# A chunked recurrence ahead of two dense layers: Gram products later, one subtraction moved to TensorE, copies in another order

## The chip, the cores and the metric

One NeuronCore of a Trainium2 chip runs the whole program. Its engines work from queues of their own and wait for each other by semaphores: TensorE (PE; its weight loads are PEld), VectorE (DVE), ScalarE (ACT), GpSimd (POOL) and SyncE (SP), which issues the DMAs. The metric is the device time of one execution in microseconds (us), median of several.

## What is computed

Three layers follow each other. For 4 batches, 8 heads, 768 tokens and a head size of 48, the first keeps a 48 x 48 state per head:

```python
k_n = k / (norm(k) + 1e-6)
for t in range(768):
    y[t]  = q[t] @ state
    v_old = k_n[t] @ state
    state = state + beta[t] * outer(k_n[t], v[t] - v_old)
```

The second takes x (the heads side by side, 384 wide): `theta = x @ w_theta`, `u = x + w_tok_r @ (x cos theta) + w_tok_i @ (x sin theta)`, `u + relu(u @ w_ch)`. The third is a layer norm with a two-layer network of width 1536 and a residual. Inputs and outputs are float32; some weights come as 64-bit floats and are rebuilt on the chip.

## The kernel before

**Chunks.** The recurrence is done in 24 chunks of 32 tokens, for 32 heads (batch x head) at once, in two halves h of 16. Within a chunk the tokens are coupled by the Gram matrix of their keys; its triangular inverse `PT`, once per group s of 4 chunks (6 groups), is computed from the keys alone. For chunk c and half h the steps are: `R` (TensorE forms K S, S being the state, and a subtraction gives `Rs = V - K S`), `W_mm` (PT times Rs), `W_out` (four ScalarE copies to `bdw`), `S` (TensorE adds K^T W to the state in PSUM, and two ScalarE copies give `bds` for the next chunk). `yq_work` and `ym_work` form the output Y, one ScalarE copy takes it to `ys`, and four DMAs take it to x.

**Gram products.** `a_work(c)` is the set for chunk c: 16 products on TensorE, two ScalarE copies (to `G_sb` for the inverse and to `MT` for the output), a mask on GpSimd. The first eight chunks' sets are made ahead of the loop. `spread` loads the keys in block form (`bdk`) two chunks ahead of a set.

**Inverse.** `inverse_work(s)` gives three lists (A, B, C) of DVE instructions, with some products on GpSimd: a transposition of the Gram blocks (`tg`, from `G_sb` to `Gi`, only when the sets of all four chunks are done), norms with a ScalarE square root between DVE instructions, the rows of 8 x 8 inverses, the steps to 16 and 32, and the transposition to `PT`. `Stream` hands them out: each half of a chunk calls `dv.run(budget)`, which emits instructions until their written-down cost passes the budget; list C of one group is mixed with list A of the next as far as that one is ready, and what a run can't emit is not carried over. In the fourth chunk of a group, and in chunk 18, the rest is emitted until PT of the next group exists.

**Order on the engines.** Each engine runs its instructions in the order in which the program writes them. In chunk c: K S of half 0 and its subtraction, inverse work, part of a Gram set, S of half 1 of the chunk before, W of half 0, Y of the chunk before, K S of half 1 and its subtraction, inverse work, the rest of the Gram set, S of half 0, W of half 1. From chunk 18 on, `late(c, k)` puts in the first work of the next layer at three places of a chunk: weights are loaded and rebuilt on DVE (`wts.step`: two instructions or three), and two tiles are prepared (`trans`, `theta`, `angles`, `sines`, `cosines`, `turn`, `rest`: x is transposed by TensorE and copied to xh and xl, its sines and cosines times x are zf, split into zh and zl). After the attention the loop over 24 tiles `mix(i, half)` begins on TensorE, with the preparation of later tiles and weights between.

Of the kernel before, what the change touches and what calls it, by code (L numbers as in the profile page):

```python
# [6 lines left out]
F32 = mybir.dt.float32  # L7
# [85 lines left out]
def attention(ctx, tc, kq, ktok, vin, betai, maskin, x, psa, late=None):  # L93
# [20 lines left out]
    beta = cst.tile([128, NS, 32], F32, name="beta")  # L114
    NB = 3
# [128 lines left out]
    def inverse_work(s):  # L244
# [10 lines left out]
        def op(n, fn, w=None, wait=0.13):  # L255
            (w or A).add(0.068 + n / 960.0, fn, wait)
# [19 lines left out]
        def n2():  # L276
            for nm in ("s1", "sh", "rc", "n", "bp", "nb"):
                nrm[nm] = sm(nm)
            v.tensor_scalar(out=nrm["s1"], in0=nrm["s0"], scalar1=1e-30, scalar2=None, op0=ALU.max)

        n2.ready = lambda: ("n1", s) in done
        op(32, n2, wait=0.4)
        op(192, lambda: v.reciprocal(out=nrm["rc"], in_=nrm["s1"]))
        op(32, lambda: v.tensor_scalar(out=nrm["sh"], in0=nrm["s1"], scalar1=0.5, scalar2=1e-6, op0=ALU.mult, op1=ALU.add), wait=0.0)
# [18 lines left out]
        A.add(0.0 if s > 1 else 0.33, lambda: (nc.gpsimd if s > 1 else v).tensor_tensor(out=N8, in0=g8[:, :, :, 0:8],  # L303
# [127 lines left out]
    def R(h, c):  # L431
        if c == 0:
            return V[0][:, 4 * h:4 * h + 4, :]
        b = bds[h][c % 2]
        for g in range(2):
            for r in range(4):
                nc.tensor.matmul(RW[h][32 * r:32 * r + 32, 0, 2 * g:2 * g + 2, :], KQ[c][:, 0, 2 * h + g, r, :],
                                 b[:, 4 * g + r, :, :], start=True, stop=True)
        Rs = p2.tile([128, 4, D], F32, name=f"Rs{h}")
        nc.vector.tensor_tensor(out=Rs, in0=V[c][:, 4 * h:4 * h + 4, :], in1=RW[h][:, 0, :, :], op=ALU.subtract)  # L440
        return Rs
# [75 lines left out]
    one = ecst.tile([128, 1], F32, name="one")  # L517
# [86 lines left out]
    for c in range(1, NC):  # L604
        s = c // 4
        step[0] = c
        load_kq(c + 11)
        load_v(c + 5)
        scale_v(c + 2)
        load_kt(c + 2)  # L610
        wa, wm, wq = Work(), Work(), Work()
        for n in {1: (9, 10), 2: (11, 12)}.get(c, (c + 10,)):
            if n < NC:
                a_work(wa, n)
        ym_work(wm, c - 1)
        yq_work(wq, c)
        R0 = R(0, c)
        budget = 2.3 if c >= 14 else 3.08
        if c % 4 == 1 and c > 1 and s + 1 < NS:
            while ("tg", s + 1) not in done:  # L620
                dv.step()
        dv.run(budget)
        if late:
            late(c, 0)
        wa.run((0.0 if c == 2 else 0.42) * wa.left())
        S(1, c - 1)
        W(0, c, R0)
# [24 lines left out]
    pe.flush()
# [472 lines left out]
def build(tc, a):  # L1125
# [8 lines left out]
    with tc.manual_schedule(), outer:  # L1134
        gp = outer.enter_context(tc.tile_pool(name="glob", bufs=1, **R))
        ident = gp.tile([128, 128], F32, name="ident")
        ones = gp.tile([128, 128], F32R, name="ones")
# [53 lines left out]
        with ExitStack() as att:  # L1191
            attention(att, tc, a["kq"], a["ktok"], a["vin"], a["betai"], a["mask"], x, psa, late)
# [4 lines left out]
        ff.ones = ones  # L1197
# [150 lines left out]
```

## Time and profile before

| | us |
|---|---|
| median of 3 runs (lowest, highest) | 784.87 (784.21, 785.08) |
| profiled execution, its own time | 786.73 |
| its span in the trace | 784.80 |
| busy: PE, DVE, ACT, POOL | 709.4, 517.8, 356.9, 213.2 |
| mean granted clock of PE | 0.969 |

The span is from the first to the last instruction in the trace; what the time has beyond it lies outside of the instructions. Busy times of engines overlap, so they don't add up to the span.

### The profile page before, as it was taken

The page shows a single profiled execution, that of the slowest core. Times are in us where ns is not written, and L with a number is a line of the kernel's source. Part 1 is how long each engine was busy: PE and PEld are TensorE (multiplying, and loading weights), DVE is VectorE, ACT ScalarE, POOL GpSimd, SP SyncE. Part 2 cuts the span into 40 slices and gives each one's busy share as a digit, 9 for nine tenths or more (in the row PEclk, how much of TensorE's full clock was granted, in tenths as well). Part 3 has the DMA queues.
Part 4 walks back from the last instruction along what each step waited for, and adds up shares of the span by engine and source line. Part 5 has one row for each costly group of instructions (what it writes and reads, how often), then busy time and mean ns, then how long its engine had stood idle before and what let it go on. Part 6 is the DMA issues. An engine that isn't in the chain of part 4 may idle for free.

```text
span 784.8 us, 18939 instructions
## 1 busy us (share of the span) xinstructions
PE 709.4 (90%) x7955; PEld 655.4 (84%) x7956; DVE 517.8 (66%) x875; ACT 356.9 (45%) x785; POOL 213.2 (27%) x234
## 2 busy tenths in 40 slices
PE   4577887777778999999997999999999999999997
PEld 3455555554468999999997999999999999999997
DVE  7987989986877888888876755435353534444342
ACT  2276776786775766654444433131322222131211
POOL 5854755744020001211111433113131221121120
PEclk8699999999989999999999999999999999999999
DMA  8975767234444223532432220000000000000000
GB/s 250 248 225 172 201 189 214 83 86 137 153 152 162 88 75 101 165 118 80 121 101 81 101 81 5 26 1 31 1 31 1 31 1 30 1 9 24 1 31 30
DMA packets 29716, 71.39 MB, mean 91 GB/s; under 512 B 4928, under 2 KB 17472, under 8 KB 29632
## 3 DMA queue, kind: packets, MB, share of 16 engines
q1 hardware_dynamic: 29632, 70.19, 29.0%
q8 instruction: 62, 1.02, 0.6%
q14 instruction: 22, 0.18, 0.1%
HBM read 56.02 MB, written 9.44 MB: 83 GB/s over the span
## 4 chain that ended last, share of the span: by engine, by line
PE 64%; DVE 15%; DMA 6%; ACT 6%; issue 5%; POOL 2%; SPq 1%; ACTq 0%; DVEq 0%; POOLq 0%
PE ph L1071 19%; PE acc L1090 19%; PE y L957 11%; PE pc L1012 5%; PE pth L897 3%; DMA bdk<-kq 3%; DVE prod L369 2%; ACT bdw L458 2%; DMA raw<-wtok 2%; PE py L492 1%; PE S L466 1%; PE pa L174 1%; DVE t L797 1%; PE RW L452 1%; DVE Ti L378 1%
## 5 line engine op out<-in xcount | busy, mean ns | idle before, releaser
L957 PE MATMUL y<-w,zh 128*128 128x384 f32 x576 | 154.8, 342 | 3.4 <-DVE u L966 2.4
L1090 PE MATMUL acc<-hh,f 128*128 128x384 f32 x576 | 147.0, 336 | 0.0
L1076 DVE SCALAR_TENSOR_TENSOR hl<-ph,hh 128x384 fp32r<-128x384 f32 x96 | 52.4, 553 | 114.5 <-ACT hh L1075 114.5
L1075 ACT ACTIVATE hh<-ph 128x384 fp32r<-128x384 f32 x96 | 46.7, 491 | 163.0 <-PE ph L1071 163.0
L1071 PE MATMUL ph<-xh,f 128*128 128x384 f32 x576 | 116.4, 337 | 0.4 <-DVE u L966 0.4
L957 PEld LDWEIGHTS y<-w,zh 128*128 128x128 f32 x576 | 105.8, 190 | 4.2 <-issue 2.7
L1090 PEld LDWEIGHTS acc<-hh,f 128*128 128x128 f32 x576 | 104.5, 188 | 0.0
L1071 PEld LDWEIGHTS ph<-xh,f 128*128 128x128 f32 x576 | 101.9, 188 | 0.7 <-issue 0.7
L957 PE MATMUL y<-w,zl 128*128 128x384 f32 x288 | 97.7, 339 | 2.4 <-DVE zl L938 2.4
L1090 PE MATMUL acc<-hl,f 128*128 128x384 f32 x288 | 96.9, 336 | 0.0
L1071 PE MATMUL ph<-xl,f 128*128 128x384 f32 x288 | 65.7, 336 | 0.0
L458 ACT COPY bdw<-RW 32x192 f32<-32x192 f32 x192 | 59.5, 310 | 13.6 <-PE RW L452 11.0
L957 PEld LDWEIGHTS y<-w,zl 128*128 128x128 f32 x288 | 54.6, 190 | 3.0 <-DVE zl L938 3.0
L471 ACT COPY bds<-S 48x384 f32<-48x384 f32 x92 | 43.5, 472 | 29.0 <-PE S L466 27.4
L466 PE MATMUL S<-bdw,ktt 128*48 128x192 f32 x368 | 42.0, 351 | 14.4 <-ACT bdw L458 14.3
L1090 PEld LDWEIGHTS acc<-hl,f 128*128 128x128 f32 x288 | 54.0, 188 | 0.0
L806 POOL TENSOR_TENSOR t<-t,g 128x384 f32<-128x384 f32 x12 | 15.3, 1279 | 135.3 <-DVE t L798 123.3
L1071 PEld LDWEIGHTS ph<-xl,f 128*128 128x128 f32 x288 | 51.6, 188 | 0.0
L452 PEld LDWEIGHTS RW<-Rs,pt 32*32 32x32 f32 x1472 | 19.8, 109 | 36.6 <-DVE Rs L440 28.5
L452 PE MATMUL RW<-Rs,pt 32*32 32x48 f32 x1472 | 26.4, 210 | 21.4 <-DVE Rs L440 21.0
L466 PEld LDWEIGHTS S<-bdw,ktt 128*48 128x48 f32 x368 | 20.8, 128 | 28.7 <-ACT bdw L458 22.2
L1100 POOL TENSOR_TENSOR o<-u,o 128x384 f32<-128x384 f32 x21 | 20.8, 1017 | 85.0 <-DVE o L1099 85.0
(165 smaller groups left out, 1305.8 us busy)
## 6 DMA issues: line engine op xcount, KB each, us to landing
kqt<-kq SPq DMA_DIRECT2D x20, 512.0 KB, 5.5
raw<-wtok SPq DMA_DIRECT2D x12, 768.0 KB, 4.7
raw<-wff SPq DMA_DIRECT2D x12, 768.0 KB, 4.9
bdk<-kq SPq DMA_DIRECT2D x40, 192.0 KB, 4.0
vt<-vin SPq DMA_DIRECT2D x24, 192.0 KB, 4.9
ktt<-ktok SPq DMA_DIRECT2D x24, 192.0 KB, 4.6
x<-ys SPq DMA_DIRECT2D x96, 48.0 KB, 2.5
flat<-t SPq DMA_DIRECT2D x12, 384.0 KB, 5.5
```

The lines of the kernel that those rows point to most:

```text
L452: nc.tensor.matmul(RW[h][rr, 1, j, :], PT[c // 4][rr, m0 + j, :], Rs[rr, j, :], start=True, stop=True)
L458: nc.scalar.copy(out=b[rr, :, r, :], in_=RW[h][rr, 1, :, :])
L466: nc.tensor.matmul(S_ps[h][64 * e:64 * e + D, g, :], KT[c][:, 2 * h + g, e, :], b[:, 2 * g + e, :, :], start=(c == 0 and g == 0), stop=Tru ...
L471: nc.scalar.copy(out=n[ee, :, e, :], in_=S_ps[h][ee, :, :].rearrange("p g (r d) -> p (g r) d", r=4))
L897: nc.tensor.matmul(ps, l[:, k], self.tw[w][:, k], start=(n == 0), stop=(n == 8))
L957: nc.tensor.matmul(self.Y[q], l[:, ri, 128 * k:128 * k + 128], self.W[s][w][:, 2 * ri + h], start=(first and w == ri == 0 and l is zh), st ...
L1012: nc.tensor.matmul(ps, self.wc[w][:, k, 128 * e:128 * e + 128], r[:, k], start=(n == 0), stop=(n == 8))
L1071: nc.tensor.matmul(ps, w[:, 0, 128 * k:128 * k + 128], r[:, k], start=(n == 0), stop=(n == 8))
L1075: nc.scalar.activation(out=hh, in_=ps, func=AF.Relu)
L1076: nc.vector.scalar_tensor_tensor(out=hl, in0=ps, scalar=0.0, in1=hh.bitcast(F32), op0=ALU.max, op1=ALU.subtract)
L1090: nc.tensor.matmul(self.ACC[j][e], w[:, 1, 128 * e:128 * e + 128], r, start=(f == 0 and n == 0), stop=(f == NF - 1 and n == 2))
L1100: (nc.vector if j == NJ - 1 else nc.gpsimd).tensor_tensor(out=o, in0=u[:, e], in1=o, op=ALU.subtract)
```

## The change

- A Gram set is made 8 chunks ahead (one per chunk) where it was 10, with two sets in chunks 1 and 2. The budget of inverse work falls from 3.08 to 2.3 at chunk 16 in place of 14. Pools that followed the last Gram set are closed and opened at chunk 15 in place of 13.
- For half 1 of chunks 1 to 18 a product of minus the identity with V is put into PSUM ahead of K S, and ScalarE copies the sum with scale -1. The subtraction on DVE is gone there. The identity is loaded at the start for this.
- The guard against a zero norm (a max with 1e-30 on DVE) becomes an addition of 1e-30 on ScalarE, and half the norm plus 1e-6 is formed there too. The product N8 is on DVE in all groups.
- `rest(0)` is written in chunk 23 behind its first half's weight step, the Y work of chunk 23 ahead of the last `late`, and the tile `ones` is filled after the attention.

```diff
-            v.tensor_scalar(out=nrm["s1"], in0=nrm["s0"], scalar1=1e-30, scalar2=None, op0=ALU.max)
+            nc.scalar.activation(out=nrm["s1"], in_=nrm["s0"], func=AF.Identity, bias=tiny)
+            nc.scalar.activation(out=nrm["sh"], in_=nrm["s0"], func=AF.Identity, scale=0.5, bias=eps)
...
-        A.add(0.0 if s > 1 else 0.33, lambda: (nc.gpsimd if s > 1 else v).tensor_tensor(out=N8, in0=g8[:, :, :, 0:8],
+        A.add(0.33, lambda: v.tensor_tensor(out=N8, in0=g8[:, :, :, 0:8],
...
+        full = h == 1 and c < LAST
+        if full:
+            nc.tensor.matmul(RW[h][:, 0, :, :], minus, V[c][:, 4 * h:4 * h + 4, :], start=True, stop=True)
         for g in range(2):
             for r in range(4):
                 nc.tensor.matmul(RW[h][32 * r:32 * r + 32, 0, 2 * g:2 * g + 2, :], KQ[c][:, 0, 2 * h + g, r, :],
-                                 b[:, 4 * g + r, :, :], start=True, stop=True)
+                                 b[:, 4 * g + r, :, :], start=not full, stop=True, skip_group_check=full)
         Rs = p2.tile([128, 4, D], F32, name=f"Rs{h}")
+        if full:
+            nc.scalar.activation(out=Rs, in_=RW[h][:, 0, :, :], func=AF.Copy, scale=-1.0)
+            return Rs
...
+    nc.sync.dma_start(out=ident, in_=identin)
+    nc.gpsimd.tensor_scalar(out=minus, in0=ident, scalar1=-1.0, scalar2=None, op0=ALU.mult)
...
-        for n in {1: (9, 10), 2: (11, 12)}.get(c, (c + 10,)):
-            if n < NC:
-                a_work(wa, n)
+        if c + 8 < NC:
+            a_work(wa, c + 8)
...
-        budget = 2.3 if c >= 14 else 3.08
+        budget = 2.3 if c >= 16 else 3.08
...
+        if c == NC - 1:
+            ym_work(pe, c)
+            pe.flush()
         if late:
             late(c, 2)
-    ym_work(pe, NC - 1)
-    pe.flush()
...
             if (c, k) == (18, 2):
-                nc.gpsimd.memset(ones.bitcast(F32), 1.0)
-                nc.scalar.copy(out=ones, in_=ones.bitcast(F32))
-                nc.sync.dma_start(out=ident, in_=a["ident"])
             if (c, k) == (22, 2):
                 mx.turn(0)
+            if (c, k) == (23, 0):
                 mx.rest(0)
-            if (c, k) == (23, 0):
                 mx.theta(1)
                 mx.angles(1)
...
-        ff.ones = ones
+        ff.ones = ones = lp.tile([128, 128], F32R, name="ones")
+        nc.gpsimd.memset(ones.bitcast(F32), 1.0)
+        nc.scalar.copy(out=ones, in_=ones.bitcast(F32))
```

Where instructions go is seen best in the order on an engine. On DVE, between the first subtraction of chunk 18 and that of chunk 19 (`Rs` from `RW_126`; those from `RW_127` are half 1), there stands before:

```order
L440 TENSOR_TENSOR Rs_3392<-vt,RW_126 128x192
L378 TENSOR_REDUCE XT<-prodp 128x16x4
L369 TENSOR_TENSOR prod<-R,XT 128x1024
L369 TENSOR_TENSOR prod<-R,XT 128x768
L440 TENSOR_TENSOR Rs_3456<-vt,RW_127 128x192
L378 TENSOR_REDUCE Ti_132<-prod 128x4x16 x2
L425 STREAM_TRANSPOSE pt<-Ti_132 128x32x32
L440 TENSOR_TENSOR Rs_3536<-vt,RW_126 128x192
```

and after the change:

```order
L451 TENSOR_TENSOR Rs_3390<-vt,RW_126 128x192
L374 TENSOR_TENSOR prod<-Gi,Ti_132 128x256
L383 TENSOR_REDUCE XT<-prod 128x2x8x4
L383 TENSOR_REDUCE XT<-prodp 128x2x8x4
L374 TENSOR_TENSOR prod<-R,XT 128x256 x2
...
L374 TENSOR_TENSOR prod<-Gi,Ti_132 128x768
L383 TENSOR_REDUCE XT<-prod 128x16x4 x2
L383 TENSOR_REDUCE XT<-prodp 128x16x4 x2
L374 TENSOR_TENSOR prod<-R,XT 128x1024
L374 TENSOR_TENSOR prod<-R,XT 128x768
L383 TENSOR_REDUCE Ti_132<-prod 128x4x16 x2
L430 STREAM_TRANSPOSE pt<-Ti_132 128x32x32
L451 TENSOR_TENSOR Rs_3555<-vt,RW_126 128x192
```

The steps to 16 and 32 of the last inverse (all but the first of the products of `Gi` with 256 elements) are now in chunk 18.

On DVE from the product `zf` of tile 0 to the second subtraction of chunk 23, before:

```order
L931 TENSOR_TENSOR zf<-zf,x_69 128x768
L938 TENSOR_TENSOR zl<-zf,zh 128x768
L440 TENSOR_TENSOR Rs_4058<-vt,RW_126 128x192
L777 TENSOR_SCALAR t<-raw 128x768
L787 TENSOR_SCALAR t<-t 128x768
L788 TENSOR_SCALAR t<-t 128x768
L907 SCALAR_TENSOR_TENSOR nf<-kk,pth 128x384
L440 TENSOR_TENSOR Rs_4130<-vt,RW_127 128x192
```

and after the change:

```order
L947 TENSOR_TENSOR zf<-zf,x_68 128x768
L451 TENSOR_TENSOR Rs_4076<-vt,RW_126 128x192
L793 TENSOR_SCALAR t<-raw 128x768
L803 TENSOR_SCALAR t<-t 128x768
L804 TENSOR_SCALAR t<-t 128x768
L954 TENSOR_TENSOR zl<-zf,zh 128x768
L923 SCALAR_TENSOR_TENSOR nf<-kk,pth 128x384
L451 TENSOR_TENSOR Rs_4149<-vt,RW_127 128x192
```

The difference `zl` has moved behind the first subtraction and behind three instructions of the weight step, which work on a load (`raw`).

On ACT from the last `bdw` copies of chunk 23 to the first `zh` of the next stage, before:

```order
L458 COPY bdw_2_123<-RW_127 32x4x48 x4
L813 CAST w_0_3650<-t 128x768
L922 ACTIVATE zf<-kk,halfpi 128x384
L498 COPY ys<-py 128x384
L879 CAST xh<-pt 128x384
L885 COPY u_65<-pt 128x3x128
L932 CAST zh<-zf 128x768
```

and after the change:

```order
L469 COPY bdw_2_123<-RW_127 32x4x48 x4
L509 COPY ys<-py 128x384
L829 CAST w_0_3669<-t 128x768
L938 ACTIVATE zf<-kk,halfpi 128x384
L1211 CAST ones<-ones 128x128
L895 CAST xh<-pt 128x384
L901 COPY u_64<-pt 128x3x128
L948 CAST zh<-zf 128x768
```

The copy `ys` now stands ahead of the cast of a weight (`w_0`) and of the cosine (`zf`), and the copy of `ones` ahead of `xh`.

## Rows read from the trace of the kernel before

**Rows 1.** The page: DVE's busy tenths in 40 slices of the span.

```profile
DVE  7987989986877888888876755435353534444342
```

**Rows 2.** Windows: length, busy of PE, PEld, DVE, ACT, POOL, clock, DMA, GB/s.

```profile
43.63:72.20 28.57, 21.64 (x624) 15.12 (x624) 22.51 (x38) 18.58 (x52) 17.02 (x22) 0.94 0.60 175
72.20:163.43 91.23, 73.87 (x2216) 51.79 (x2216) 83.09 (x172) 66.09 (x184) 52.76 (x65) 0.94 0.60 170
103.05:109.91 6.86, 6.46 (x183) 4.81 (x184) 5.90 (x19) 4.27 (x13) 3.37 (x6) 0.75 0.70 192
163.43:177.14 13.71, 10.28 (x320) 6.78 (x320) 11.37 (x19) 12.13 (x31) 7.50 (x8) 1.00 0.30 85
177.14:185.95 8.81, 5.84 (x168) 3.82 (x168) 8.04 (x9) 6.40 (x18) 5.78 (x8) 1.00 0.32 87
185.95:192.29 6.34, 5.67 (x152) 3.92 (x152) 2.26 (x7) 3.76 (x11) 2.49 (x5) 0.73 0.58 195
```

**Rows 3.** Timeline of ACT, chunks 13 to 16: start us, us, instruction [idle before].

```profile
145.19 0.48 ACT L498 COPY ys<-py 128x384 f32<-128x384 f32 x1
...
146.13 0.97 ACT L471 COPY bds<-S 48x384 f32<-48x384 f32 x2
...
162.73 1.27 ACT L458 COPY bdw<-RW 32x192 f32<-32x192 f32 x4
...
165.01 0.97 ACT L471 COPY bds<-S 48x384 f32<-48x384 f32 x2 [1.01 <-PE S L466]
...
166.01 1.27 ACT L458 COPY bdw<-RW 32x192 f32<-32x192 f32 x4
```

**Rows 4.** Timeline of DVE: prologue, and last a row of chunk 5.

```profile
15.68 0.23 DVE L312 TENSOR_TENSOR prod<-N,Ti 128x64 f32<-128x64 f32 x1
...
18.26 0.98 DVE L369 TENSOR_TENSOR prod<-Gi,Ti 128x256 f32<-128x256 f32 x2
...
20.39 0.97 DVE L369 TENSOR_TENSOR prod<-R,XT 128x256 f32<-128x256 f32 x2
...
27.17 1.00 DVE L378 TENSOR_REDUCE XT<-prodp 128x64 f32<-128x512 f32 x2
...
33.34 0.67 DVE L378 TENSOR_REDUCE Ti<-prodp 128x64 f32<-128x512 f32 x1
...
34.51 2.11 DVE L425 STREAM_TRANSPOSE pt<-Ti 128x1024 f32<-128x1024 f32 x1 [0.50 <-POOL mt L216]
...
82.67 0.97 DVE L369 TENSOR_TENSOR prod<-R,XT 128x256 f32<-128x256 f32 x2 [0.68 <-ACT R L327]
```

**Rows 5.** Timeline of PE, end of chunk 2.

```profile
60.95 0.27 PE L481 MATMUL py<-bds,kqt 128*32 128x96 f32 x2 [1.68 <-issue]
```

**Rows 6.** Timeline of DVE, ACT and POOL, chunk 23 and after.

```profile
223.76 0.62 DVE L777 TENSOR_SCALAR t<-raw 128x768 uint32<-128x768 uint32 x1 [1.24 <-DMA raw<-wtok]
...
225.95 0.35 DVE L440 TENSOR_TENSOR Rs<-vt,RW 128x192 f32<-128x192 f32 x1
...
228.58 0.83 ACT L813 CAST w<-t 128x768 fp32r<-128x768 f32 x1
...
229.32 0.61 ACT L922 ACTIVATE zf<-kk,halfpi 128x384 f32<-128x384 f32 x1
...
229.49 2.03 POOL L820 TENSOR_TENSOR w<-t,w 128x768 fp32r<-128x768 f32 x1 [5.53 <-ACT w L813]
...
230.15 0.48 ACT L498 COPY ys<-py 128x384 f32<-128x384 f32 x1 [0.22 <-PE py L492]
...
230.97 0.48 ACT L879 CAST xh<-pt 128x384 fp32r<-128x384 f32 x1 [0.34 <-PE pt L870]
```

**Rows 7.** Chain that ended last, and two timeline rows of ACT and PE.

```profile
236.71 4.17 DMA raw<-wtok
...
240.96 0.90 ACT L781 ACTIVATE t<-raw 128x768 f32<-128x768 f32 x1 [3.36 <-DMA raw<-wtok]
...
250.38 0.44 PE L957 MATMUL y<-w,zl 128*128 128x384 f32 x1 [1.89 <-DVE zl L938]
```

More of the change, by code (lines that the diff above doesn't have):

```diff
@@ L90, in step, with attention @@
         return False
-def attention(ctx, tc, kq, ktok, vin, betai, maskin, x, psa, late=None):
+LAST = 19
+def attention(ctx, tc, kq, ktok, vin, betai, maskin, identin, ident, x, psa, late=None):
     nc = tc.nc
@@ L114, in attention @@
     beta = cst.tile([128, NS, 32], F32, name="beta")
+    minus = cst.tile([128, 128], F32, name="minus")
     NB = 3
@@ L269, in n1 @@
         def n1():
-            nrm["s0"] = sm("s0")
+            for nm in ("s0", "s1", "sh"):
+                nrm[nm] = sm(nm)
             nc.scalar.activation(out=nrm["s0"], in_=diag, func=AF.Sqrt)
+            nc.scalar.activation(out=nrm["s1"], in_=nrm["s0"], func=AF.Identity, bias=tiny)
+            nc.scalar.activation(out=nrm["sh"], in_=nrm["s0"], func=AF.Identity, scale=0.5, bias=eps)
             done.add(("n1", s))
@@ L276, in n2 @@
         def n2():
-            for nm in ("s1", "sh", "rc", "n", "bp", "nb"):
+            for nm in ("rc", "n", "bp", "nb"):
                 nrm[nm] = sm(nm)
-            v.tensor_scalar(out=nrm["s1"], in0=nrm["s0"], scalar1=1e-30, scalar2=None, op0=ALU.max)
+            v.reciprocal(out=nrm["rc"], in_=nrm["s1"])
         n2.ready = lambda: ("n1", s) in done
-        op(32, n2, wait=0.4)
-        op(192, lambda: v.reciprocal(out=nrm["rc"], in_=nrm["s1"]))
-        op(32, lambda: v.tensor_scalar(out=nrm["sh"], in0=nrm["s1"], scalar1=0.5, scalar2=1e-6, op0=ALU.mult, op1=ALU.add), wait=0.0)
+        op(192, n2, wait=0.4)
         op(32, lambda: tt(out=nrm["rc"], in0=nrm["rc"], in1=diag, op=ALU.mult), wait=0.05)
@@ L516, in attention @@
     nc.vector.memset(zero, 0.0)
-    one = ecst.tile([128, 1], F32, name="one")
+    few = ecst.tile([128, 3], F32, name="few")
+    one, tiny, eps = [few[:, n:n + 1] for n in range(3)]
+    nc.vector.memset(tiny, 1e-30)
+    nc.vector.memset(eps, 1e-6)
     nc.vector.memset(one, 1.0)
@@ L642, in attention @@
         wq.flush()
-        if c == 13:
+        if c == 15:
             soon.close()
@@ L1136, in build @@
         ident = gp.tile([128, 128], F32, name="ident")
-        ones = gp.tile([128, 128], F32R, name="ones")
         g = gp.tile([128, KB], F32, name="g")
@@ L1149, in late @@
         def late(c, k):
-            if (c, k) == (13, 2):
+            if (c, k) == (15, 2):
                 xp2 = ph1.enter_context(tc.tile_pool(name="x_", bufs=1, **R))
@@ L1191, in build @@
         with ExitStack() as att:
-            attention(att, tc, a["kq"], a["ktok"], a["vin"], a["betai"], a["mask"], x, psa, late)
+            attention(att, tc, a["kq"], a["ktok"], a["vin"], a["betai"], a["mask"], a["ident"], ident, x, psa, late)
         lp = outer.enter_context(tc.tile_pool(name="left", bufs=1))
```

## The prediction, made before the changed kernel ran

> **What bounds the kernel now.** I read the busy shares by slice first [rows 1]. VectorE (DVE) is the fuller engine in the first quarter of the span, where the attention runs; from then on TensorE (PE) is full, and the change touches nothing in that later part but its start. So the question is when the attention hands over, and how soon PE is fed after that.
>
> Inside the attention I cut the span at the first subtraction (Rs of half 0) of a chunk, the only DVE instruction that every chunk waits for [rows 2]. Chunks 1 to 3 take 28.57 us, chunks 4 to 15 91.23 us (7.60 each), chunks 16 and 17 13.71, chunk 18 8.81. DVE is busy for 83.09 of the 91.23 us: the chunks' products and the inverse work share that engine, and the inverse work ends later. In chunks 16 and 17, where less of it is left, ScalarE's chain ends last: a group of bdw copies (1.27 us), a wait of 1.01 for the S products, the bds copies (0.97), and the next group 3.28 after the first [rows 3]. Two halves make 6.56 us, the floor of a chunk. The wait of 1.01 is the room in which ys and the Gram copies fit: ys at 145.19 to bds at 146.13 is 0.94 us for three copies.
>
> In chunks 1 to 3 PE itself stalls. It does two Gram sets per chunk there, and one stop of 1.68 us is put down to issue [rows 5].
>
> After the attention one chain runs through ACT, DVE and a weight load: the copy xh at 230.97, then zh and zl of the second tile, the weight rebuild, the DMA issued at 236.71, and PE's wait of 1.89 us that ends at 250.38 [rows 6, 7]. From 250.38 on PE does not wait again in this stage, so what is added to that chain is added to the end.
>
> **Chunks 1 to 3.** One Gram set per chunk replaces two, and the transposition that opens the next inverse leaves this stretch, since its Gram blocks come later. DVE keeps the rest of the first inverse, from the 64-element product on. The prologue ran the same list without subtractions: 15.68 to 36.62 (34.51 + 2.11) is 20.94 us; its 0.67 reduction of prodp is not in later inverses (GpSimd adds those), so 20.3 [rows 4]. Three Rs of 0.35 make 21.4 us. Against 28.57: -7.2 us. Bounds: -8.5 (DVE loses nothing to waits) and -4.5 (the stop of 1.68 comes back and a chunk falls on ScalarE's floor).
>
> **Chunks 4 to 15.** With a lead of 8 the Gram blocks of an inverse are complete only in the chunk before its group of four begins, and the transposition can start no earlier. So each inverse now lies in exactly four chunks and can't run ahead, as it does now. Per group:
> - First chunk: transposition, square root and norms. The list is short, but the DVE waits for ScalarE in the middle of it. Chunk 8 now has this shape, 6.86 us [rows 2]; I take 6.9. Removing the guard and the sh operation from DVE, and putting N8 on it instead of a wait for GpSimd, are inside this chunk, whose end DVE does not set: nothing. If that cover were gone, they are a few tenths.
> - Second: the rows and the first products. DVE has less to do than the floor; ScalarE's window with ys and two Gram copies gets the new Rs copy too. 0.94 plus about 0.30 (a bdw copy is a quarter of 1.27, 0.32; the three copies go by steps of 0.31) passes 1.01 by 0.23: 6.56 + 0.23, 6.8 us.
> - Third: from the R,XT products at 20.39 to the first prodp reduction of the pair that starts at 27.17, 7.3 us, an Rs, and the wait for the R copy (0.68 in chunk 5): 8.2 us, DVE last.
> - Fourth: the same list as chunk 18 now, 8.81 us, less its second Rs, which lies beside the wait for GpSimd that ends the list: 8.8.
>
> That is 30.7 per group, 92.1 for three: +0.9 us. So the 0.35 us per chunk that the second subtraction frees is not paid out: the list must be done by the end of the fourth chunk, and the two light chunks can't lend their idle time to the two heavy ones. PE's extra product (minus times V) is not in the trace. It stands ahead of PE's wait for bds and is hidden by it; not hidden, it is at most about what two R products take, 0.27 [rows 5]. Bounds: -5 (the lists of the heavy chunks fit under the light ones) and +4 (the minus product and the half clock in each group).
>
> **Chunks 16 to 18.** The last inverse starts two chunks later and at the low pace. Chunks 16 and 17 keep ScalarE's floor without Gram copies: 13.3 against 13.71, -0.4. In chunk 18 the list is flushed until its transposition is done, and the order shows that this is everything from the second 256-element product on. The prologue ran that from 18.75 (18.26 plus half of the pair's 0.98) to 36.62: 17.87, less the 0.67, plus an Rs of 0.35: 17.6 us [rows 4]. Now chunk 18 takes 8.81. +8.8 us; bounds +7 and +10. Half 1 of the chunk no longer waits for DVE, but the first subtraction of chunk 19 stands behind the whole list, and everything of chunk 19 behind it.
>
> Here one rule of the Trainium skill speaks against the change. In chunk 19 PE's granted clock is 0.73 already, after the flush in chunk 18 [rows 2]; I leave chunk 19 at its 6.34 us. "TensorE: Matmul & The Clock Gate", Part 1, says that the throttled clock is the default and that sustained activity releases it. By that, a chunk 18 with twice the idle time would leave all of chunk 19 at the low level: the 46% of 6.34 that is at 2.4 GHz now (0.54 x 0.5 + 0.46 = 0.73) could take up to twice as long, an estimate of at most +2.9 us; the trace agrees in direction.
>
> **The end of the attention.** The last difference zl of tile 0 moves from ahead of chunk 23's first subtraction to behind the weight steps there. It now fills DVE's wait for raw (1.24 us, ending at 223.76 [rows 6]); behind that wait it pushes nf and the second subtraction back by its length, about 0.9 us. The first subtraction gets earlier, but ScalarE reaches its bdw copies no sooner. +0.9 (bounds 0 and +1).
>
> The last Y copy now comes before the weight cast and the cosine. Now these two (0.83 and 0.61) fill ScalarE's wait for the last products, ys runs at 230.15 and xh at 230.97. After the change ScalarE waits through that time, copies ys, then casts, then the cosine. Behind it stands a new instruction, the copy of ones, and it waits for GpSimd's memset of ones, which is queued behind the low part of the second weight (2.03 us now, from 229.49, when the cast is done). So, from the end of the last bdw copies (228.58 now): 1.57 until ys, ys 0.48, cast 0.83, low part 2.03, memset and copy 0.25 each as an estimate (a third of the elements of ys), then xh, at 5.3 with the small overlaps off, where it is 2.39 now (230.97). +2.9 us; bounds +1 (only the cast and the cosine) and +3.8. xh is the head of the chain of [rows 7], which has no slack. Ident's load ahead of the first chunks and the minus product on GpSimd lie under memsets and loads of the prologue: 0, at most +0.3.
>
> **The sum.** -7.2 + 0.9 - 0.4 + 8.8 + 0.9 + 2.9 = +5.9 us. The profiled execution has a span of 784.80 and its own time is 786.73; the median of the runs is 784.87, which I take as the base: 790.8 us.
>
> **Rivals.**
> - Faster: the chunks 4 to 15 spread their load after all. DVE's first subtraction may come late without cost: in chunk 16 it starts at 163.43, and ScalarE reaches the copies behind it only at 166.01 [rows 2, 3], a slack of some 1.6 us once the subtraction and the W products (an estimate of 0.6) are off. If the heavy chunks live in this slack, a group of four takes the mean of DVE's and ScalarE's sums, near 28.2: 3 x 2.5 = 7.5 less, 783.3 us. It decides the sign when a group falls under 28.3. For it: half 1 no longer waits on DVE. Against: the heavy pair exceeds the floor by 3.7 us in sum, over twice the slack. 0.18.
> - No difference: the groups gain half of that and the chain after the attention hides the late xh (ScalarE waits 3.36 us for raw in it, ending at 240.96 [rows 7]): about 785. For it: ScalarE is mostly idle there; against: DVE's rebuild, not ScalarE, issues the load. 0.13.
> - Slower by more: the half clock. Chunk 8 now runs at 0.75 after PE waited for DVE [rows 2]. If every group's first chunk and chunk 19 start so, with the minus product at the low clock, +1 each: 794 to 795. 0.12.
> - The forecast: 0.57.
>
> The forecast's own range is 787.5 to 793; with the rivals 782.5 to 794.5. About 0.2% (1.6 us) is what a measurement of this kernel tells from no change: faster 0.18, same 0.14, slower 0.68.
>
> **What the profile will show.** Right: chunk 4's first subtraction near 65 us instead of 72.20; groups of 30 to 31 us with the last two chunks over 8; a chunk 18 of 17 to 18 us with DVE full and PE mostly idle; the ones copy directly ahead of the first xh of the next stage, ended by GpSimd, and PE's wait before the third tile 3 us later against the last Y product. Wrong: groups under 29 us, a chunk 18 under 14, or an xh as early after the last bdw copies as now.

## The result and the profile after

| | us |
|---|---|
| changed kernel, median of 4 runs (lowest, highest) | 793.66 (790.86, 795.31) |
| kernel before, median of 4 runs beside it | 784.98 |
| ratio, 95% interval | 1.0106 (1.0081 to 1.0132) |
| profiled execution after: own time, span | 790.86, 789.1 |
| the same kernel measured again (experiment r1, 6 runs) | 790.90 (789.51, 794.03), ratio 1.0070 (1.0048 to 1.0092) |

The change makes the kernel slower, by 5.5 us (0.0070 x 785.5) in one measurement and 8.3 us (0.0106 x 785) in the other; both intervals hold 6.4 to 7.2 us. The forecast was 5.9 us. The first median lies above the forecast's own range (787.5 to 793), the second in it. The two medians differ by 2.8 us, so a difference of that size against one of them alone says little.

The windows of the changed kernel, cut as in [rows 2] at the first subtractions of chunks (chunks 1 to 3, 4 to 15, 8, 12, 16 and 17, 18, 19); the last row runs from that of chunk 22 to the last one of the attention:

```profile
42.42:64.79 22.37, 19.93 (x584) 13.56 (x582) 20.84 (x30) 17.83 (x50) 16.48 (x20) 1.00 0.68 194
64.79:155.16 90.37, 79.53 (x2316) 53.86 (x2312) 79.79 (x139) 73.35 (x209) 51.61 (x66) 0.98 0.65 184
94.79:101.36 6.57, 5.86 (x188) 4.04 (x188) 5.56 (x13) 5.34 (x17) 1.52 (x2) 1.00 0.61 172
124.39:131.39 7.00, 6.60 (x182) 4.58 (x186) 4.79 (x13) 5.05 (x15) 1.60 (x2) 0.76 0.57 185
155.16:168.81 13.65, 11.66 (x316) 7.61 (x316) 8.10 (x27) 11.06 (x30) 2.06 (x4) 0.87 0.21 64
168.81:186.44 17.63, 6.62 (x170) 4.12 (x170) 16.40 (x19) 7.38 (x20) 9.60 (x11) 0.79 0.15 41
186.44:193.69 7.25, 6.81 (x154) 4.81 (x156) 2.37 (x6) 3.90 (x11) 2.50 (x5) 0.56 0.50 158
212.66:228.20 15.54, 10.24 (x233) 6.95 (x233) 13.33 (x17) 11.98 (x28) 3.69 (x2) 0.85 0.35 116
```

Chunks 1 to 3 are 6.2 us shorter (22.37, 28.57 before). Chunk 18 is 8.8 us longer (17.63, 8.81 before): DVE is busy for 16.40 us of it and PE for 6.62. The third and fourth row are the first chunks of two groups of four (chunks 8 and 12): the same work, at a granted clock of 1.00 and of 0.76.

What PE does in chunk 18, three rows of its timeline show (start, length, instruction, idle time before and what ended it):

```profile
176.03 0.86 PE L477 MATMUL S<-bdw,ktt 128*48 128x192 f32 x8 [0.76 <-ACT bdw L469]
186.83 0.86 PE L463 MATMUL RW<-Rs,pt 32*32 32x48 f32 x32 [9.94 <-DVE Rs L451]
187.62 0.87 PE L503 MATMUL py<-bdw,mt 128*32 128x192 f32 x8
```

PE has one wait of 9.94 us for the subtraction of chunk 19, which stands on DVE behind the whole list.

The end of the attention, timelines of DVE, ACT and POOL after the change, to be read beside [rows 6]:

```profile
224.26 2.10 DVE L803 TENSOR_SCALAR t<-t 128x768 f32<-128x768 f32 x1
...
228.20 0.35 DVE L451 TENSOR_TENSOR Rs<-vt,RW 128x192 f32<-128x192 f32 x1
```

```profile
232.40 0.48 ACT L509 COPY ys<-py 128x384 f32<-128x384 f32 x1 [1.59 <-PE py L503]
232.78 0.83 ACT L829 CAST w<-t 128x768 fp32r<-128x768 f32 x1
233.51 0.62 ACT L938 ACTIVATE zf<-kk,halfpi 128x384 f32<-128x384 f32 x1
235.72 0.30 ACT L1211 CAST ones<-ones 128x128 fp32r<-128x128 f32 x1 [1.60 <-POOL ones L1210]
235.93 0.47 ACT L895 CAST xh<-pt 128x384 fp32r<-128x384 f32 x1
```

```profile
224.10 1.84 POOL L836 TENSOR_TENSOR w<-t,w 128x768 fp32r<-128x768 f32 x1 [5.55 <-ACT w L829]
233.69 1.86 POOL L836 TENSOR_TENSOR w<-t,w 128x768 fp32r<-128x768 f32 x1 [7.74 <-ACT w L829]
235.49 0.21 POOL L1210 MEMSET ones<- 128x128 f32 x1
```

The queue stands as forecast: ScalarE waits 1.59 us for the last product, copies ys, casts the weight and forms the cosine; then it waits 1.60 us for GpSimd, whose memset stands behind the low part of the weight. From the last subtraction to xh it is 7.73 us (228.20 to 235.93); before it was 5.02. What was not forecast is the first row: a DVE instruction of 2.10 us.

### The profile page after: what moved, and what is told of

Its sections match the earlier page's. It is cut to its first block, busy times and chain, and to the rows that moved or that the text cites. A ratio compares the mean times of both kernels' runs of the same rounds, so it can differ in the third digit from the quotient of the medians.

```text
span 789.1 us, 18969 instructions
## 1 busy us (share of the span) xinstructions
PE 720.1 (91%) x7992; PEld 659.6 (84%) x7992; DVE 518.1 (66%) x851; ACT 362.4 (46%) x815; POOL 209.6 (27%) x231
## 3 DMA queue, kind: packets, MB, share of 16 engines
q1 hardware_dynamic: 29632, 70.19, 28.7%
## 4 chain that ended last, share of the span: by engine, by line
PE 63%; DVE 18%; ACT 6%; issue 5%; POOL 5%; DMA 3%; SPq 0%; ACTq 0%; DVEq 0%; POOLq 0%
PE ph L1087 19%; PE acc L1106 19%; PE y L973 11%; PE pc L1028 5%; DVE prod L374 3%; PE pth L913 3%; DVE XT L383 2%; DMA raw<-wtok 2%; ACT bdw L469 2%; POOL prodp L374 2%; POOL prodp L390 1%; PE py L503 1%; DVE zl L954 1%; PE RW L463 1%; PE S L477 1%
## 5 line engine op out<-in xcount | busy, mean ns | idle before, releaser
L469 ACT COPY bdw<-RW 32x192 f32<-32x192 f32 x192 | 59.4, 310 | 20.4 <-PE RW L463 17.6
L482 ACT COPY bds<-S 48x384 f32<-48x384 f32 x92 | 43.5, 473 | 20.4 <-PE S L477 19.2
```

What stands on the lines that cost most here:

```text
L469: nc.scalar.copy(out=b[rr, :, r, :], in_=RW[h][rr, 1, :, :])
L482: nc.scalar.copy(out=n[ee, :, e, :], in_=S_ps[h][ee, :, :].rearrange("p g (r d) -> p (g r) d", r=4))
```

## The experiments

Times are medians, ratios are to the kernel before on the same chip. Runs r1 to r4 were on one chip, r5 to r8 on a second and r9 to r12 on a third, so between these sets the ratio is the safer comparison. Every edit is to the changed kernel unless it says otherwise.

**r1: the changed kernel again.**

> The changed kernel once more, unaltered, for a second trace and more times (four so far: 790.9, 793.3, 794.0 and 795.3 us, the trace being of the first). If the program itself sets the pieces, the chunk lengths of the trace (chunks 1 to 3 22.4, chunk 18 17.6, last subtraction to first xh 7.7 us) come again within 0.3 us, and what runs differ by lies in the dense layers after 250 us or in the granted clock. Rival: the spread of 4 us lies in the attention, as another arrival of loads, and chunk lengths differ by 1 us or more.

790.90, ratio 1.0070 (1.0048 to 1.0092). Windows of its trace (chunks 1 to 3, 4 to 15, the first chunks of two groups, chunk 16, chunk 18):

```profile
44.45:67.34 22.89, 20.91 (x606) 14.20 (x598) 20.64 (x30) 18.23 (x52) 15.87 (x20) 0.99 0.67 201
67.34:158.48 91.14, 81.09 (x2316) 54.61 (x2312) 79.59 (x140) 73.34 (x209) 51.58 (x66) 0.98 0.65 184
97.67:104.83 7.16, 6.78 (x182) 4.83 (x186) 4.77 (x14) 4.95 (x15) 1.53 (x2) 0.76 0.69 192
128.57:135.05 6.48, 5.82 (x182) 4.01 (x182) 5.47 (x13) 5.31 (x18) 1.58 (x2) 1.00 0.79 220
158.48:164.10 5.62, 4.78 (x154) 3.27 (x154) 4.18 (x12) 4.47 (x14) 0.26 (x1) 1.00 0.10 30
170.90:188.51 17.61, 6.63 (x170) 4.12 (x170) 16.38 (x19) 7.38 (x20) 9.60 (x11) 0.80 0.16 41
```

Chunk 18 and the way to xh (7.73 again) come back to 0.02 us; chunks 1 to 3 don't come within the 0.3 us expected (22.89 and 22.37). What varies more is the prologue (first subtraction at 42.42 and 44.45), which group's first chunk runs at 0.76 (here chunk 8, there chunk 12), and chunks 16 and 17 (12.42 and 13.65; chunk 16 is 5.62 at a clock of 1.00 here and 6.56 at 0.74 there). So part of the spread lies in the attention, as the rival said.

**r2: the last inverse spread over three chunks.**

```diff
-        budget = 2.3 if c >= 16 else 3.08
+        budget = 4.2 if 16 <= c <= 18 else 2.3 if c > 18 else 3.08
```

> The changed kernel with a budget of 4.2 in chunks 16 to 18 (2.3 there now), so that the last inverse is spread over three chunks in place of a flush in chunk 18. Theory (the flush costs 8.8 us because DVE works alone): chunks 16, 17, 18 take 6.9, 9.5 and 10.6 us, 27.0 in sum where they take 31.3, and the time falls by 4.3 us against the repeat. Rival: the late work of chunks 19 to 23 waits for its weight loads and gives it back, under 1 us less; another rival: the three chunks stay at 31 us, since ScalarE and DVE alternate.

786.80, ratio 1.0015 (0.9998 to 1.0033): 4.1 us under r1. Chunks 16, 17, 18 and 19:

```profile
157.54:165.43 7.89, 7.45 (x154) 4.65 (x154) 5.53 (x20) 4.75 (x15) 0.27 (x1) 0.57 0.11 26
165.43:174.74 9.31, 6.50 (x170) 4.13 (x170) 8.83 (x17) 8.72 (x21) 5.95 (x7) 1.00 0.24 69
174.74:185.82 11.08, 5.57 (x162) 3.69 (x162) 10.51 (x11) 5.18 (x14) 6.21 (x8) 0.95 0.18 55
185.82:192.75 6.93, 6.40 (x152) 4.39 (x152) 2.37 (x6) 3.67 (x11) 2.50 (x5) 0.59 0.53 166
```

Chunks 16 to 18 take 28.28 us (31.28 in the first trace, 30.03 in r1; 27.0 expected), with chunk 16 at half the clock for most of it, and PE's wait ahead of chunk 19 is 4.73 us. The traced execution, 791.37, is the longest of the twelve, and chunks 19 to 21 give 1 us back in it (27.27, and 26.2 in the two traces of the changed kernel), as DVE waits 2.33 us for weights' loads (raw) in chunk 21, and 1.07 and 1.02 in those two. So this trace as a whole does not show the 4.1 us; by the time, and by the same budget in r5 below (chunks 16 to 18 27.41, 19 to 21 26.14), the flush is the larger part of the loss, and it is a matter of where the list is cut.

**r3, r4, r10: the end of the attention, taken back in parts.** r3 has the last Y work behind the cast and the cosine again and fills ones in the mix loop; r10 only the second of these; r4 only rest(0).

```diff
# r3 (both), r10 (the second)
-        if c == NC - 1:
-            ym_work(pe, c)
-            pe.flush()
...
+    ym_work(pe, NC - 1)
+    pe.flush()
# ones: from behind the attention to behind the third tile of the mix
+            if i == 2:
+                nc.gpsimd.memset(ones.bitcast(F32), 1.0)
+                nc.scalar.copy(out=ones, in_=ones.bitcast(F32))
# r4
                 mx.turn(0)
+                mx.rest(0)
             if (c, k) == (23, 0):
-                mx.rest(0)
```

> The changed kernel with the last Y work behind the last weight cast and cosine again, and with the fill of ones moved into the mix loop (after its third tile). Theory: from the end of the last bdw copies to the first xh it is 2.4 us where it is 5.1, the chain behind it has no slack, and the time falls by 2.7 us. Rival: the wait of 3.4 us for raw in that chain hides it, and the time is the same within 1 us. If only one of the two moves matters, xh comes 1 us earlier, not 2.7.

> The changed kernel with only the fill of ones moved into the mix loop; the last Y work stays ahead of the cast and the cosine. Theory: xh stands behind the cosine then, which ends 4.6 us after the start of the last bdw copies (1.27, a wait of 1.59, 0.48, 0.83, 0.62 less overlaps), so xh comes at 4.6 where it is 6.4 in the changed kernel and 3.7 in the one with both undone: 1.8 of the 2.7 us are the fill waiting behind GpSimd's low part, 0.9 the order of Y. Time -1.8 against the repeat. Rival: xh still waits for its own transposition on TensorE, and nothing is gained.

> The changed kernel with rest(0) back in chunk 22 behind its turn. Theory: the weight cast on ScalarE and GpSimd's low part come 2 us earlier, so the DVE instruction that took 2.10 us beside GpSimd's low part (0.56 before the change) is short again; chunk 23's first to second subtraction falls from 5.86 to 3.8 us, and the time by 2.1 us. Rival: only the move of zl counts and the long DVE instruction has another cause and stays: 0.9 us less. Other rival: the DVE waits for raw instead, no change.

r3: 789.26, ratio 1.0049 (1.0033 to 1.0066), 1.6 us under r1 where 2.7 were expected. r10: 792.25, 1.0071 (1.0048 to 1.0095), no different from r1 where 1.8 were expected. r4: 790.86, 1.0059 (1.0039 to 1.0079), 0 to 0.9 us under it (by medians, by ratios) where 2.1 were expected. All three intervals overlap that of r1, so the times alone do not show these terms. In the traces the mechanisms are plain. ACT's last bdw copies and xh in r3, then in r10:

```profile
232.36 1.27 ACT L469 COPY bdw<-RW 32x192 f32<-32x192 f32 x4 [0.28 <-PE RW L463]
...
236.04 0.48 ACT L894 CAST xh<-pt 128x384 fp32r<-128x384 f32 x1 [0.34 <-PE pt L885]
```

```profile
231.90 1.28 ACT L469 COPY bdw<-RW 32x192 f32<-32x192 f32 x4
...
235.88 0.62 ACT L938 ACTIVATE zf<-kk,halfpi 128x384 f32<-128x384 f32 x1
236.40 0.47 ACT L895 CAST xh<-pt 128x384 fp32r<-128x384 f32 x1
```

From the start of these copies to xh: 3.68 in r3 (3.69 before), 4.50 in r10, 6.40 in the changed kernel. So in the traces the fill of ones is 1.9 of the 2.7 us and the order of Y 0.8, as expected; the order of before also gives 3.05 us (r6, r8) and 3.36 (r11), so a few tenths of it vary. In r4 chunks 22 and 23 up to the last subtraction take 14.14 us, as before (211.81 to 225.95), where they take 15.54 and 15.36 in the two traces of the changed kernel; GpSimd's low part ran from 225.25 to 227.13, and the DVE instruction that was long is short (the one ahead of it, which began beside the low part, took 1.27 us):

```profile
227.58 0.56 DVE L803 TENSOR_SCALAR t<-t 128x768 f32<-128x768 f32 x1
```

But no time is as much lower as its trace up to xh, and r9 shows what can happen behind xh.

**r9: the kernel before with only the three edits at the end.**

```diff
# before
+        if c == NC - 1:
+            ym_work(pe, c)
+            pe.flush()
...
-                nc.gpsimd.memset(ones.bitcast(F32), 1.0)
-                nc.scalar.copy(out=ones, in_=ones.bitcast(F32))
...
-                mx.rest(0)
             if (c, k) == (23, 0):
+                mx.rest(0)
```

(with ones filled behind the attention)

> The kernel before with only the three edits at the end: rest(0) in chunk 23, the last Y work ahead of the last cast and cosine, and ones filled after the attention. The attention up to chunk 22 is unaltered. Theory: chunks 22 and 23 take 15.0 to 15.5 us in sum where they take 14.1, the first xh comes 6.4 us after the start of the last bdw copies where it is 3.7, and the time rises by 3.6 to 4 us. Rival (from the times, in which the edits at the end taken back gave 1.7 and 0 to 2 us): +2 us, part of it hidden behind the wait for raw; if hidden wholly, no change.

788.83, ratio 1.0024 (1.0005 to 1.0042): slower, by 1.9 us as the ratio has it and 3.3 as the medians do (785.50); 3.6 to 4 were expected, and 2 by the rival. In the trace chunks 22 and 23 take 14.95 (+0.8) and xh comes 6.41 after the start of the last bdw copies (+2.7). From xh to the end it is 552.67 us, and 553.83 before: 1.2 us come back. Two windows show where: from xh to the matmul with which PE resumes after zl [rows 7], and 9.6 us from there. Before, then r9, then the second window alone of r2, which has the end of the changed kernel:

```profile
230.97:250.38 19.41, 16.73 (x97) 16.07 (x96) 14.83 (x20) 10.61 (x18) 0.55 (x1) 1.00 0.43 155
250.38:260.00 9.62, 9.62 (x47) 9.58 (x48) 8.33 (x14) 6.02 (x11) 0.00 (x0) 0.82 0.36 142
```

```profile
234.53:253.73 19.20, 16.05 (x86) 15.32 (x84) 14.85 (x20) 10.74 (x19) 0.00 (x0) 0.91 0.47 176
253.73:263.35 9.62, 9.62 (x56) 9.59 (x57) 8.33 (x14) 5.94 (x11) 0.00 (x0) 1.00 0.40 144
```

```profile
255.13:264.75 9.62, 9.62 (x47) 9.59 (x48) 8.33 (x14) 6.02 (x11) 0.00 (x0) 0.82 0.38 146
```

Before, PE waits 1.89 us ahead of that matmul, and then does 47 matmuls at a granted clock of 0.82. In r9 it waits 0.35 us and then does 56 at 1.00; its clock has fallen earlier. From that matmul to the end of the span it is 534.42 us before and 533.47 in r9. So the trace of r9 is 2.3 us longer from chunk 22 on (0.8 + 2.7 - 1.2), between ratio and medians. With the end of the changed kernel 0.7 us come back in its first trace, 1.1 in r1 and 0.7 in r12, whose clocks fall early too. But r2 and r7, which have that end as well, wait 1.89 us and take 553.84 and 553.82 from xh to the end, as before; and among the traces with the order of before that stretch runs from 552.81 (r8) to 554.37 (r6). So what comes back is not shown to come from the edits: it goes with where PE's clock falls in an execution, and what decides that was not found.

**r8, r7, r12: the parts of the attention.** r8 is the kernel before with the lead of 8 chunks, the switch at 16 and the closing at 15 alone; r7 the changed kernel with half 1's subtraction on DVE; r12 the changed kernel with the guard and N8 as before.

```diff
# r8 (before)
-        for n in {1: (9, 10), 2: (11, 12)}.get(c, (c + 10,)):
-            if n < NC:
-                a_work(wa, n)
+        if c + 8 < NC:
+            a_work(wa, c + 8)
-        budget = 2.3 if c >= 14 else 3.08
+        budget = 2.3 if c >= 16 else 3.08
# r7
-LAST = 19
+LAST = 0
# r12
-            nc.scalar.activation(out=nrm["s1"], in_=nrm["s0"], func=AF.Identity, bias=tiny)
-            nc.scalar.activation(out=nrm["sh"], in_=nrm["s0"], func=AF.Identity, scale=0.5, bias=eps)
+            v.tensor_scalar(out=nrm["s1"], in0=nrm["s0"], scalar1=1e-30, scalar2=None, op0=ALU.max)
```

> The kernel before with the lead of 8 chunks, the budget switch at chunk 16 and the closing at 15 alone (both subtractions on DVE, guard and tail as before). Theory: chunks 1 to 3 give 6 us, chunk 18 takes 9 us more, groups of four 31 us (+1.5 for the subtractions in the heavy chunks) and the end is as before: +4 us against before. Rival: without the product by TensorE the early gain is gone as well, +8; other rival: chunk 18 is what costs and the groups get shorter, +1.

> The changed kernel with the half-1 subtraction on DVE again in all chunks (no minus product). Theory of the prediction (the list must be done by the end of the fourth chunk and what the subtraction frees on DVE is not paid out except in the heavy chunks): the third and fourth chunk of each group and chunk 18 get 0.35 us longer, chunks 1 to 3 0.3 each, the light chunks shorter by up to 0.3 as TensorE has less; in all +1 to +3 us. Rival: half 1 waiting for DVE behind its inverse work is a wait of its own, over 1 us per heavy chunk, +8 us or more. Other rival: the minus product costs TensorE more than DVE gains, -2 us.

> The changed kernel with the guard as before: max and half norm on DVE, N8 by GpSimd from the third inverse on. Theory of the prediction: nothing (within 0.5 us), since the end of the first chunk of a group is not set by DVE's list. Rival: the two more ScalarE instructions between square root and DVE cost 0.5 us in each first chunk and give it back here, -2 us; other rival: the wait for GpSimd's N8 comes back, +0.5 us in each of three groups, +1.5.

r8: 791.91, ratio 1.0076 (1.0049 to 1.0103): the lead alone costs 6 us, where 4 were expected (its span is 3.0 us above the one before). r7: 793.94, 1.0105 (1.0082 to 1.0129). r12: 793.43, 1.0085 (1.0062 to 1.0108). Chunks 1 to 3, 4 to 15 and 18 of r8:

```profile
42.59:67.23 24.64, 18.56 (x596) 13.19 (x588) 22.19 (x34) 17.75 (x50) 17.07 (x21) 1.00 0.73 205
67.23:157.96 90.73, 74.88 (x2282) 53.55 (x2284) 82.67 (x155) 67.78 (x189) 52.77 (x67) 0.94 0.62 181
170.86:189.08 18.22, 6.04 (x168) 3.82 (x168) 17.02 (x20) 7.63 (x20) 10.64 (x14) 0.80 0.14 40
```

The first two of r7, and chunks 1 to 3 and chunk 4 of r12:

```profile
43.59:65.92 22.33, 17.41 (x576) 12.75 (x576) 21.08 (x33) 16.20 (x46) 15.65 (x20) 1.00 0.64 191
65.92:156.44 90.52, 74.01 (x2284) 52.59 (x2284) 83.06 (x152) 69.04 (x195) 51.72 (x65) 0.96 0.65 185
```

```profile
44.23:69.04 24.81, 21.18 (x606) 14.23 (x598) 21.58 (x30) 18.81 (x54) 16.84 (x21) 1.00 0.72 200
69.04:74.85 5.81, 5.43 (x186) 4.02 (x186) 4.71 (x14) 4.88 (x15) 1.26 (x2) 1.00 0.61 189
```

- Chunks 4 to 15 take 90.5 us with the subtraction on DVE (r7), 90.4 and 91.1 with TensorE's product, and 90.7 with none of the other edits (r8). DVE is busy for 83.06 us in r7 and 79.79 after: 3.3 us of DVE time were freed there, and none was paid out, as far as single traces tell (the two of the changed kernel differ by 0.8). The rows show where some of it went: in the third chunk of a group DVE waits 0.69, 0.68 and 0.68 us for ScalarE's copy R in the first trace (0.39, 0.68 and 0.67 in r1), and 0.36, 0.42 and nothing in r7. Third chunks take 8.40 to 8.42 us in the first trace and 7.68 to 8.14 in r7, fourth ones 8.57 to 8.62 and 8.86 to 9.04: the pair is 17.0 us in either kernel (16.7 in the last group of r7 and the first of r1).
- r7 is 3 us above r1 in time, but only 0.3 above the first measurement of the changed kernel, and its interval overlaps those of both. In its trace chunk 18 accounts for 0.6 (18.22), and chunk 21 for 2.4 (13.07 at a granted clock of 0.74; 10.68 at 1.00 in r1). Chunk 21 has the same work in both; DVE waits there 2.26 us for a weight's load (raw), and 1.02 in r1. So whether the subtraction gains anything in time stays open.
- The guard was costed at nothing, and r12 shows it in chunks 1 to 4: 30.62 us in sum, and 29.14 and 29.67 in the two traces of the changed kernel (r7, with the new guard and the old subtraction, has 29.04; r8, with neither, 30.48). With the guard on DVE, the rest of list C that is emitted at the end of chunk 3 is longer, as the order of the two kernels has it (from the last reduction ahead of the products R,XT of 1024 and 768 elements, in place of the second of these), and chunk 3 takes 8.59 where r1 has 7.00. It is not the operations' own time but the place where the budget cuts the list. In time the two can't be told apart (793.43, against 793.66 and 790.90).

**r5, r6, r11: together, and with other budgets.** r5 has r2, r3 and r4 together. r6 and r11 have also other budgets inside each group of four:

```diff
-        budget = 2.3 if c >= 16 else 3.08
+        budget = {16: 5.6, 17: 4.0, 18: 4.0}.get(c, (4.6, 2.8, 2.6, 3)[c % 4] if c < 16 else 2.3)   # r6
+        budget = {16: 5.6, 17: 4.0, 18: 4.0}.get(c, (3.5, 3.3, 2.6, 3)[c % 4] if c < 16 else 2.3)   # r11
```

> The three edits of the runs before together: budget 4.2 in chunks 16 to 18, the last Y work behind the cast and the cosine with ones filled in the mix loop, rest(0) in chunk 22. Theory (separate terms that add up): -4.1 for the flush as the times showed, -2.7 and -2.1 for the two at the end as the traces showed, 8.9 us under the repeated changed kernel: 782, and under the kernel before by 3.5. Rival (the times of the second and third edit count, -1.7 and 0): 785, no different from before.

> As r5_all, and the budgets inside each group of four are 4.6, 2.8, 2.6 and a flush in place of 3.08 and a flush (DVE lists of 6.1, 6.2, 6.3 and 7.4 us by the rows of the trace, where they are 4.7, 5.5, 7.9 and 7.9), and 5.6 and 4.0 in chunks 16 and 17. Theory (the heavy chunks end with DVE, the light ones do not, so moving work to the light ones is free): groups of 28.9 us where they take 30.0 to 30.9, 3.3 to 5 us less than r5_all. Rival: the light chunks are full already by TensorE (6.07 busy of 6.19) and what is added there is added to the time: groups stay at 30, no difference to r5_all.

> As r6_balance with budgets 3.5, 3.3, 2.6 and a flush inside each group (DVE lists of 5.1, 6.7, 6.7 and 7.4 us where r6 had 6.1, 6.2, 6.3 and 7.4). Theory (the first chunk of a group can't take more work, as its DVE waits 1 to 2 us for ScalarE's square root, and took 8.1 to 9.05 us in r6; the second and third can): groups of 29.3 us where r6 has 29.2 to 30.5, and 1 to 2 us less time than r6. Rival: what leaves the first chunk is added to the second and third in full, groups of 30, time as r6 (782.4).

r5: 784.97, ratio 0.9995 (0.9980 to 1.0011), no different from before, as its rival had it (785, and not 782); the separate times add up (-4.1, -1.6 and 0 to -1), the traces' larger terms don't. r6: 782.43, 0.9957 (0.9943 to 0.9971). r11: 783.03, 0.9972 (0.9955 to 0.9989). Both are faster than both kernels, r6 by 0.43% than before. One group of four of r6, and of r11:

```profile
96.12:105.16 9.04, 8.04 (x212) 4.98 (x204) 6.64 (x19) 6.64 (x20) 1.57 (x2) 1.00 0.59 174
105.16:111.54 6.38, 5.66 (x188) 4.10 (x190) 6.00 (x16) 5.59 (x17) 3.11 (x6) 1.00 0.75 233
111.54:118.17 6.63, 6.29 (x192) 4.37 (x194) 6.63 (x8) 5.61 (x16) 5.79 (x5) 1.00 0.74 214
118.17:126.24 8.07, 7.42 (x214) 4.90 (x204) 7.93 (x7) 6.16 (x18) 6.96 (x10) 1.00 0.71 210
```

```profile
96.83:103.90 7.07, 6.23 (x192) 4.28 (x192) 5.78 (x16) 6.30 (x19) 1.57 (x2) 1.00 0.76 208
103.90:110.94 7.04, 6.37 (x194) 4.21 (x190) 6.52 (x20) 5.78 (x17) 2.78 (x5) 1.00 0.77 222
110.94:117.89 6.95, 6.41 (x194) 4.45 (x194) 6.92 (x9) 5.80 (x17) 6.16 (x6) 1.00 0.74 204
117.89:125.98 8.09, 7.43 (x214) 4.89 (x202) 7.94 (x7) 6.13 (x18) 6.94 (x9) 1.00 0.69 210
```

In r6 what the heavy chunks lose the first one takes: 30.12 us, where 28.9 were expected. In r11 this group is 29.15 us, near the 29.3 expected (the other two 30.56 and 29.16), and still its time is not 1 to 2 us under r6's, as expected, but 0.6 above. That r6 is 2.5 us under r5 the traces don't show (chunks 4 to 15: 89.87 and 89.27). One difference is that no first chunk of these groups ran at 0.76 in r6 and r11 (chunks 8 and 12 of both traces), while in the seven traces with the changed kernel's budgets there (after, r1 to r5, r10) it did in five of fourteen. r5's own trace has none of the five; whether its other executions do was not seen, so the cause stays open.

## Why the prediction was right, and where it was off

The direction and the two large terms came out by the mechanisms that were forecast; that the sum came so near is in part luck, as terms that were off by 1 us and more have opposite signs. The terms, by the prediction's own steps, in the two traces of the changed kernel against the trace of before (rounded each):

| step | forecast | first trace | r1 |
|---|---|---|---|
| up to the first subtraction | 0 | -1.2 | +0.8 |
| chunks 1 to 3 | -7.2 | -6.2 | -5.7 |
| chunks 4 to 15 | +0.9 | -0.9 | -0.1 |
| chunks 16, 17 | -0.4 | -0.1 | -1.3 |
| chunk 18 | +8.8 | +8.8 | +8.8 |
| chunks 19 to 21 | 0 | +0.4 | +0.4 |
| chunks 22, 23 to the last subtraction | +0.9 | +1.4 | +1.2 |
| last subtraction to xh | +2.9 | +2.7 | +2.7 |
| xh to the end | 0 | -0.7 | -1.1 |
| sum | +5.9 | +4.3 | +5.8 |

- **Chunk 18** was right in mechanism and size (17.6 forecast, 17.63 and 17.61), because the order gave the list and the prologue had run it. r2 and r5 confirm it by undoing it.
- **Chunks 1 to 3**: the right mechanism, over-sized by 1 to 1.5 us. The step took the time of the prologue's list and three subtractions, and allowed for no wait of DVE on the rest of a chunk. DVE is busy 20.84 us there and idle for 1.5; in r1 20.64 and 2.3. (It also put two Gram sets into each of the three chunks; chunk 3 had one.) Part of the gain comes with the guard's edit (r8 and r12: 24.6 and 24.8, of which chunk 4 has 1 us back), by another cut of the list, and none with the move of the subtraction (r7: 22.33). The step "inside this chunk: nothing" failed for the guard, since it looked at the operations and not at what their cost does to the budget.
- **Chunks 4 to 15**: 30.0, 29.6 and 30.8 us a group (30.3, 30.9 and 29.9 in r1) where 30.7 was forecast, and as said, DVE's freed time is not paid out (r7); the step's reason, light chunks that can't lend, is not the whole of it, since in the heavy chunks, too, a longer wait for R stands against what was freed. Inside a group the step was wrong for the second chunk: 6.8 us forecast from a floor of 6.56, 6.05 and 6.19 measured in the first two groups. 6.56 is no floor of a chunk: chunk 16 takes 5.62 in r1, and chunks 4 and 14 took 5.95 and 6.06 in the trace of before. The heavy pair, 17.0, was forecast rightly. The rival that they spread their load by themselves is out (28.2; by the prediction's own terms the sign would turn at 28.7, not at 28.3). The rival of the half clock is partly in: in r1 the first two chunks of a group take 13.91 us where the first is at 0.76 and 12.91 where not, so it costs 1 us, in some groups of some runs. (Not every long second chunk is the clock's: chunk 5 of r1 takes 6.87 us at 1.00.) The first measurement, 793.66, lies nearer to this rival's 794 to 795 us than to the forecast.
- **Chunk 19** was left at 6.34 us and takes 7.25 and 7.30, at a clock of 0.56 where it was 0.73. The direction is that of the rule of the Trainium skill that the prediction weighed ("TensorE: Matmul & The Clock Gate", Part 1); 0.9 us, under the bound of 2.9 given there. r2, with a shorter last wait, has 6.93 at 0.59. In the sum chunks 20 and 21 gave half of it back. The 0.9 us do not come every time: r3, behind a wait of 9.96 us, has 6.46 at 0.67 for chunk 19:

```profile
188.53:194.99 6.46, 5.82 (x152) 4.03 (x152) 2.25 (x6) 3.49 (x10) 2.50 (x5) 0.67 0.59 183
```

- **rest(0)**: 0.9 forecast for zl, 0.8 measured where nothing else happens (r9, and 14.94 to 14.96 us for chunks 22 and 23 in r2, r7 and r12 as well), and 0.4 to 0.6 more in the two traces of the changed kernel, where a DVE instruction meets GpSimd's low part (below).
- **The head of the next chain**: 2.7 us for 2.9, cut as said into the fill of ones (1.9) and the order of Y (0.8). The step that the chain has "no slack" held in r2 and r7 and not in the two traces of the table (0.7 and 1.1 us less behind xh); as r9 shows, the cause of that difference is open.

The pieces of the two traces sum to 4.3 and 5.8 us, and the measurements gave 8.3 and 5.5; what the untraced runs do beyond that is open. A part of it is which execution was traced: the one before lay 1.8 us above its median, the first one after 2.8 below, that of r1 1.5 above.

## What to carry to other kernels

A list of work that is handed out by budget has a deadline, and it is the deadline that a change of lead moves: count what is left when the flush comes, from the order, and price it with rows of a stretch that ran the same list alone. Time freed on one engine by work for another can come back as a wait for the other: 0.35 us a chunk left DVE here, and the pair of heavy chunks stayed at 17.0. When an instruction is put ahead of a copy that others wait for, look at what the engine that feeds it has queued: 0.5 us of filling a tile delayed xh by 1.9 in the traces. And two medians of one kernel differed by 2.8 us here: measure the changed kernel twice before an edit is priced against it.

## What the runs showed of the hardware beyond what was expected

- **DVE beside GpSimd.** Around the end of the attention, DVE's instructions of 0.56 us (128 x 768, one input and one or two scalars) took 1.65 to 2.30 us in thirteen traces where they began 0.03 to 0.6 us behind the start of GpSimd's low part (1.8 to 2.3 us, two inputs), 0.60 to 1.58 where they began 0.7 to 1.7 us behind it, and 0.55 to 0.59 where they began with it or ahead of it. In the first trace of the changed kernel three were so long, at 209.73, 216.74 and 224.26; before it was one, at 208.78, and one with two inputs at 215.98 (2.55 us, 0.96 elsewhere). Such an instruction ends 0.41 to 0.43 us after GpSimd does (224.10 + 1.84 = 225.94; 224.26 + 2.10 = 226.36). The Trainium skill says of the pair of ports that GpSimd shares with DVE's two-port modes, which such an instruction can enter ("SBUF — State Buffer", Who interferes with whom), that the one that issues first has it for its whole instruction, and the other is blocked, not slowed. The trace agrees: the length is GpSimd's remainder plus 0.42 us, less than the instruction's own 0.56.
- **Where a clock falls can matter.** In the two windows above (before and r9), PE's granted clock falls once either way: to a mean of 0.82 over 9.6 us in which PE is busy throughout, or to one of 0.91 over 19.2 us in which it is idle for 3.2. From the matmul that ends the wait to the end of the span, the second is 0.95 us shorter. The other traces of the same end agree: 553.84 and 553.82 us from xh to the end with the late fall (r2, r7), 552.67 to 553.17 with the early one (the changed kernel twice, r9, r12).
